# A searched order for the first 640 steps, and products of zeros in nearly all TensorE waits of the opening, in an attention and gated-MLP kernel

## The chip, the core and the metric

One core of a Trainium2 chip runs the whole kernel. The time is device microseconds of one execution; a verdict rests on several executions of both kernels on the same chip. The kernel before took 577.91 us (median of 3 runs, 577.79 to 578.27).

## What is computed

Attention over 8 batches, 8 heads, 576 positions and 64 channels, then a gated MLP on its output, all in float32:

```python
scores = scale * np.matmul(q, k.transpose(0, 1, 3, 2))
mask = (rel >= 0) & (rel < 128)
scores = np.where(mask, scores + bias, -1e9)         # bias = -slope(h) * |rel|
attn = softmax(scores); x = attn @ v                 # heads side by side: 576 x 512
h = gelu_tanh(x @ w_in); u, v = halves of h
v_s = w_sg @ layer_norm(v, g_ln) + b_sg[:, None]     # mixes positions
out = x + (u * v_s) @ w_out
```

The products of the MLP are done in three float32r products each (high by high, high by low, low by high); the weights come as 64-bit words and are first split into a high and a low float32r part.

## The kernel before

The work is cut into named steps. 32 pairs of heads (four of a batch) each go through the same attention steps; the letter is the step, the number is the pair:

- q, L: loads of q and k, and of v, issued by SP
- a, c (for pairs 5 and on together as *): score matmuls of the first and second half (TensorE, line 278)
- A, B, C, G: masks, bias and row minima (VectorE, lines 302 and 295)
- e, E, f, F, j: exponentials (ScalarE, line 311), with their row sums
- R: reciprocals of the row sums (VectorE, lines 322 and 323)
- s, S, r: scaling (ScalarE, line 329, or GpSimd, line 334)
- t, T, z: transposes (TensorE, lines 347 and 360); X, Y: their masked copies (VectorE, line 356); P: a small copy (ScalarE)
- V: products with v (TensorE, lines 384 and 388)
- x, p: gather on ScalarE (line 393); 2: gather on VectorE (line 396; step "22" is pair 2's, "20" pair 0's, "21" pair 1's)
- h, l, k: high and low part of the MLP's input (ScalarE line 401, GpSimd line 218, ScalarE)

The weights w_in are split by six steps each (number 0 to 7; 8 to 11 are w_out): i load (line 181), d on ScalarE (lines 192 and 194), b and o on VectorE (lines 196 and 198), + on GpSimd (line 218), H on ScalarE (line 203), and - on GpSimd (line 218) for even numbers, on VectorE (line 208) for odd ones. wl, wH and w- do the same for w_sg.

Of the MLP of batch 0, the second half of the hidden layer comes first: w20 and its like are the product of position block 2 with the input rows of pair 0, v02 is the last of a block's four (lines 607 to 609, 512 columns wide, reads h and l); vg is its gelu (line 786), nv..., vn... its norm. u000, u001 and so on are the products of the first half (lines 607 to 609, 288 wide), ug0 its gelu, tt0 to tn0 the last 64 positions, y020 and so on the products with w_sg.

W0, W1 and so on are products of zeros: a 128 by 128 block of a tile of zeros times 288 columns of it, into a PSUM buffer that nobody reads.

```python
for i in range(n):
    at = i // len(banks) % 2 * (512 - S2)
    nc.tensor.matmul(banks[i % len(banks)][:, at:at + S2], spare[:, 0:P], spare, start=True, stop=True)
```

The order of all steps is one written list, the table ORDER. A loop at the end takes its steps one after the other and emits their instructions; each engine, and the queue of loads and stores on SP, gets its instructions in this order and runs them in this order. So a step waits for its data and for a free buffer, and everything behind it on its engine waits as well. The buffers that matter here: two of each of three PSUM pools (ps_s, ps_a of one bank, ps_m of two), two of qk, two of vt, four staging buffers for weights (wst).

```python
for n, run in plan.run(ORDER.split()):
    run()
    for i in nc.cur_bb.bb.instructions[before:]:
        if i.engine in last:
            tc.add_manual_dep(i, last[i.engine], ..., reason="order")
        last[i.engine] = i.name
```

Of the kernel before, what the change touches and what calls it, by code (L numbers as in the profile page):

```python
# [21 lines left out]
def attention_gmlp(  # L22
# [26 lines left out]
    S2 = S // 2  # L49
# [8 lines left out]
    IDLE = [(12, "ps_a"), (4, "ps_a"), (4, "ps_s"), (4, "ps_s"), (4, "ps_a"), (4, "ps_m"), (4, "ps_m"), (3, "ps_m"), (4, "ps_m"), (4, "ps_m"), (2, "ps_m"), (2, "ps_m")]  # L58
# [6 lines left out]
    ps_s = ctx.enter_context(tc.tile_pool(name="ps_s", bufs=2, space=PSUM))  # L65
    ps_a = ctx.enter_context(tc.tile_pool(name="ps_a", bufs=2, space=PSUM))
# [100 lines left out]
    gb = const.tile([P, F], F32, name="gb")  # L167
# [978 lines left out]
    for b in range(B):  # L1146
# [4 lines left out]
        q0 i2 d2 i1 q1 a0 c0 A0 a1 i0 B0 C0 G0 b2 c1 e0 d1 E0 F0 j0 f0 d0 b1 o2 o1 +2 A1 R0 B1 C1 b0 o0 G1 L0 i5 q3 i3  # L1151
        j1 H2 s0 E1 e1 f1 r0 F1 d3 S0 +0 +1 -2 W0 t0 X0 W5 T0 Y0 W2 W4 z0 R1 b3 o3 P0 r1 V0 z1 H0 p0 s1 H1 x0 a3 A3 B3
        t1 20 X1 c3 C3 G3 -0 +3 S1 T1 W9 wl2 wH2 P1 w-2 i6 q2 d5 d6 H3 h0 wl3 L1 i7 q5 L2 F3 j3 e3 E3 f3 d7 a2 b5 b6
        o5 +5 l0 Y1 A2 B2 R3 o6 -3 -1 b7 W11 W8 W3 V1 s3 w20 t3 W10 W6 x1 p1 j2 e2 21 h1 +6 S3 X3 c2 l1 w30 T3 W7 w00
        w21 E2 wH3 C2 f2 G2 F2 r3 z3 w-3 H6 P3 Y3 R2 s2 -6 o7 S2 +7 L3 i9 i4 gb i10 V3 x3 23 p3 k1 H5 r2 h3 w01 t2 w10
        T2 X2 Y2 l3 w31 w11 z2 d4 d10 P2 V2 x2 H7 p2 b4 o4 b10 o10 22 +4 +10 w13 w33 *5 A5 B5 C5 G5 w03 w23 h2 H4 d9
        l2 v03 v02 v00 v01 W1 e5 j5 vg03 H10 vg02 vg00 vg01 -5 b9 o9 -7 -4 nv30b nv00b nv10b -10 +9 nv00p u000 u030
        u001 F5 k0 H9 nv10c nv00c -9 E5 nv00h f5 k3 nv30c vn00 L5 i11 q7 i8 wl1 q4 tl R5 a4 u031 A4 B4 s5 t5 nv20b r5
        z5 uc00 wH1 k2 tH uc03 j4 E4 w-1 nv10p S5 nv20p t- e4 nv10h X5 c4 C4 f4 G4 P5 F4 bl L4 wl0 tt0 T5 u020 Y5 R4
        vn01 tj0 s4 r4 u021 V5 t4 nv20c u010 tg0 d11 nt0b nv30p x5 p5 wH0 S4 nt0p w-0 X4 25 T4 z4 u011 Y4 nv20h uc02  # L1160
        nv30h P4 bH nt0c vn03 b- vn02 V4 nt0h x4 d8 p4 uc01 tn0 b11 o11 b8 24 o8 y020 y021 *7 +11 ug0 A7 +8 B7 y000
        y001 H11 j7 H8 Us0 C7 G7 -11 -8 Us1 gm02 gm00 F7 E7 f7 e7 q9 q6 L6 *6 A6 R7 gh00 gh02 h4 B6 C6 e6 q8 L7 s7
        y010 y011 t7 S7 gl02 r7 T7 y030 G6 gm01 X7 F6 E6 f6 j6 R6 gl00 s6 S6 Y7 y031 z7 gm03 gh01 h5 P7 V7 p7 gh03
        gl01 t6 T6 X6 Y6 Oa0 x7 gl03 r6 O00 z6 27 oa00 Us2 l4 l5 P6 h7 V6 p6 x6 Us3 26 O01 h6 l6 l7 *8 oa01 A8 B8 C8
        Us4 G8 u100 u101 e8 *9 E8 f8 j8 F8 R8 A9 B9 u110 s8 S8 r8 t8 C9 k4 k7 Uh1 uc10 E9 j9 f9 e9 k5 k6 Ul1 X8 G9
# [105 lines left out]
```

## Time and profile before

| | |
|---|---|
| time, median of 3 runs | 577.91 us (577.79 to 578.27) |
| the profiled execution, span from first to last instruction | 577.4 us |
| mean granted TensorE clock | 0.997 |
| TensorE matmul busy | 560.8 us, 97%, 5495 matmuls |
| VectorE busy | 473.8 us, 82% |
| ScalarE busy | 378.6 us, 66% |
| GpSimd busy | 308.0 us, 53% |
| the chain that ended last | TensorE 90%, VectorE 5%, DMA 2%, ScalarE 1% |

The page gives the span of the profiled execution and no other time of it; the median of the runs lies 0.5 us over that span. PE is TensorE, DVE is VectorE, ACT is ScalarE, POOL is GpSimd. The granted clock is a share of 2.4 GHz, so 0.50 is 1.2 GHz. In a time line a row gives start, duration, engine, line, operation and tiles, and in brackets the idle time ahead of it with what ended that; matmuls overlap, so a row of several is a little longer than the time to the next row. The opening, up to some 57 us, is where TensorE has idle time and where the products of zeros stand; behind it TensorE is busy nearly throughout.

### The profile page before, as it was taken

What the parts mean: (1) busy time and instruction counts of PE and PEld (TensorE: products, weight loads), DVE (VectorE), ACT (ScalarE), POOL (GpSimd) and SP (SyncE); (2) the same over time, 40 slices, a digit from 0 to 9 for tenths busy, and PEclk for the clock granted to TensorE, in tenths of its full rate; (3) what the DMA queues carried; (4) which work ended last, traced back from release to release, by engine and by line L of the source; (5) the groups of instructions that cost most, each with busy time, mean ns of one, the idle gap of its engine ahead of it and who ended that gap; (6) DMA issues with size and microseconds to landing.
All of it is one profiled execution on the core that took longest, in us unless ns stands there. A gap on an engine that the chain in (4) does not pass through costs nothing.

```text
span 577.4 us, 14654 instructions
## 1 busy us (share of the span) xinstructions
PE 560.8 (97%) x5495; PEld 512.7 (89%) x5495; DVE 473.8 (82%) x1324; ACT 378.6 (66%) x1063; POOL 308.0 (53%) x365
## 2 busy tenths in 40 slices
PE   5889999999999999999999999999999999999997
PEld 4667899998899799997999998998989999998997
DVE  7989998799989868899788987878897988666646
ACT  7988997466853867467776576746695667833422
POOL 3676646530436543575447753496347653576325
PEclk9989999999999999999999999999999999999999
DMA  8675213216403413454260465135332606012502
GB/s 297 190 235 199 72 45 121 69 46 243 167 37 125 156 37 99 146 192 129 60 212 10 140 204 173 43 103 168 130 120 65 214 2 197 2 35 96 171 1 82
DMA packets 43561, 69.78 MB, mean 121 GB/s; under 512 B 3554, under 2 KB 31202, under 8 KB 43492
## 3 DMA queue, kind: packets, MB, share of 16 engines
q1 hardware_dynamic: 43492, 68.86, 36.7%
q8 instruction: 43, 0.70, 0.5%
q14 instruction: 26, 0.21, 0.1%
HBM read 56.27 MB, written 12.58 MB: 119 GB/s over the span
## 4 chain that ended last, share of the span: by engine, by line
PE 90%; DVE 5%; DMA 2%; ACT 1%; issue 1%; POOL 0%; SPq 0%; DVEq 0%; ACTq 0%
PE ps_m L607 13%; PE ps_m L1059 13%; PE ps_m L609 12%; PE ps_m L608 12%; PE ps_m L905 12%; PE ps_a L347 5%; PE ps_s L384 4%; PE ps_s L278 4%; PE ps_a L278 4%; PE ps_m L384 3%; DMA qk<-qkT 2%; PE ps_m L941 2%; PE ps_m L940 1%; DVE px L356 1%; DVE e L295 1%; PE ps_m L796 1%
## 5 line engine op out<-in xcount | busy, mean ns | idle before, releaser
L334 POOL TENSOR_TENSOR e<-e,rr 128x256 f32<-128x256 f32 (+2 forms) x116 | 80.7, 718 | 97.0 <-DVE rr L323 84.9
L311 ACT ACTIVATE e<-e,stats 128x128 f32<-128x128 f32 (+1 forms) x288 | 110.6, 386 | 17.7 <-DVE stats L295 17.1
L224 POOL TENSOR_TENSOR region<-u,region 128x288 fp32r<-128x288 f32 (+1 forms) x78 | 77.7, 1016 | 44.7 <-ACT region L1006 16.2
L356 DVE TENSOR_TENSOR px<-ps_a,m_both 128x1024 f32<-128x1024 f32 x64 | 77.4, 1216 | 5.9 <-PE ps_a L347 5.4
L607 PE MATMUL ps_m<-ws,region 128*128 128x288 f32 x256 | 78.2, 306 | 0.0
L609 PE MATMUL ps_m<-ws,region 128*128 128x288 f32 x256 | 75.7, 296 | 0.0
L608 PE MATMUL ps_m<-ws,region 128*128 128x288 f32 x256 | 75.6, 295 | 0.0
L730 POOL TENSOR_TENSOR rs<-rs,mhalf 128x1 f32<-128x1 f32 (+1 forms) x40 | 30.2, 756 | 57.4 <-DVE rs L727 57.2
L218 POOL TENSOR_TENSOR xs<-xf,xs 128x288 fp32r<-128x288 f32 (+1 forms) x48 | 49.9, 1060 | 13.8 <-ACT xs L401 13.8
L311 ACT ACTIVATION_READ_ACCUMULATOR e<-e,stats 128x1 f32 x288 | 54.4, 189 | 0.0
L1006 ACT ACTIVATE region<-u 128x576 fp32r<-128x576 f32 x35 | 23.7, 684 | 43.4 <-PE ps_m L608 17.4
L607 PEld LDWEIGHTS ps_m<-ws,region 128*128 128x128 f32 x256 | 48.3, 189 | 1.5 <-issue 0.8
L608 PEld LDWEIGHTS ps_m<-ws,region 128*128 128x128 f32 x256 | 48.2, 188 | 0.1
L609 PEld LDWEIGHTS ps_m<-ws,region 128*128 128x128 f32 x256 | 48.1, 188 | 0.1
L607 PE MATMUL ps_m<-wi,xs 128*128 128x512 f32 x112 | 46.9, 418 | 0.1
L1066 DVE TENSOR_TENSOR xf<-ps_m,xf 128x576 f32<-128x576 f32 x48 | 35.7, 750 | 10.9 <-PE ps_m L1059 10.1
L609 PE MATMUL ps_m<-wi,xs 128*128 128x512 f32 x112 | 44.3, 395 | 0.0
L608 PE MATMUL ps_m<-wi,xs 128*128 128x512 f32 x112 | 44.2, 395 | 0.0
L946 DVE TENSOR_TENSOR u<-ps_m,u 128x576 f32<-128x576 f32 x32 | 24.0, 752 | 18.7 <-PE ps_m L941 11.5
L347 PE MATMUL ps_a<-ident,e 128*128 128x128 f32 x256 | 38.0, 275 | 1.0 <-DVE px L356 1.0
L295 DVE CUSTOM_DVE_ANT_0 e<-ps_s,bias 128x128 f32<-128x128 f32 (+1 forms) x140 | 34.9, 287 | 2.5
L278 PE MATMUL ps_s<-qk 64*64 64x192 f32 (+2 forms) x576 | 31.5, 333 | 5.3 <-DMA qk<-qkT 4.9
(217 smaller groups left out, 1600.9 us busy)
## 6 DMA issues: line engine op xcount, KB each, us to landing
qk<-qkT SPq DMA_DIRECT2D x32, 576.0 KB, 4.7
sum<-store SPq DMA_DIRECT2D x36, 512.0 KB, 4.8
outT<-xf SPq DMA_DIRECT2D x31, 288.0 KB, 3.0
vt<-v_in SPq DMA_DIRECT2D x32, 256.0 KB, 4.1
wst<-w_in SPq DMA_DIRECT2D x8, 512.0 KB, 4.8
store<-sum SPq DMA_DIRECT2D x6, 512.0 KB, 2.7
vt<-v_in SPq DMA_DIRECT2D x64, 32.0 KB, 4.2
wst<-w_out SPq DMA_DIRECT2D x4, 512.0 KB, 3.6
```

Of the source, the lines that this page charges most:

```text
L218: (engine or nc.gpsimd).tensor_tensor(out[:, cs], a[:, cs], b[:, cs], op)
L224: nc.gpsimd.tensor_tensor(out[:, fs], a[:, fs], b[:, fs], ALU.subtract)
L278: return lambda: nc.tensor.matmul(banks[half][to, c:c + k1 - k0], qk[js, 0, q0:q0 + R], qk[js, 1, k0:k1], start=True, stop=True)
L311: nc.scalar.activation(x, x, AF.Exp, bias=self.nm[0:n, i:i + 1], scale=-1.0, accum_out=self.sm[0:n, i:i + 1])
L334: nc.gpsimd.tensor_tensor(x[:, z:z + step, :], y[:, z:z + step, :], self.rr[0:n, i + z:i + z + min(k, step)].rearrange("p (m o) -> p m o", ...
L347: burst([lambda t=t: nc.tensor.transpose(cv[:, t // 2, t % 2], self.pr[j][:, t, :].rearrange("p (h c) -> p h c", h=2), ident[:, j * R:j * ...
L356: nc.vector.tensor_tensor(xv, cv, mv, ALU.mult)
L607: nc.tensor.matmul(dst, ah, bh, start=(first and i == 0), stop=False)
L608: nc.tensor.matmul(dst, ah, bl, start=False, stop=False)
L609: nc.tensor.matmul(dst, al, bh, start=False, stop=(last and i == n - 1))
L905: nc.tensor.matmul(dst, left(n, g, c)[:, ms], right(n, h, c), start=first and c == 0 and k == 0, stop=c == 1 and k == 2, skip_group_check= ...
L1059: nc.tensor.matmul(dst, p, q, start=first and f == 0 and k == 0, stop=f == 1 and k == 2, skip_group_check=True)
```

## The change

Two tables change, no step's own code. IDLE says how many products of zeros each W step has and in which pool: 12 steps with 51 products become 24 steps with 85. ORDER puts the first 640 or so steps, up to about 165 us of the span, in another order; the remaining 1363 steps stand as before.

```diff
-    IDLE = [(12, "ps_a"), (4, "ps_a"), (4, "ps_s"), (4, "ps_s"), (4, "ps_a"), (4, "ps_m"), (4, "ps_m"), (3, "ps_m"), (4, "ps_m"), (4, "ps_m"), (2, "ps_m"), (2, "ps_m")]
+    IDLE = [(4, "ps_m"), (4, "ps_m"), (5, "ps_m"), (1, "ps_m"), (4, "ps_a"), (4, "ps_a"), (4, "ps_a"), (4, "ps_a"), (4, "ps_a"), (5, "ps_a"), (2, "ps_m"), (1, "ps_m"), (4, "ps_m"), (4, "ps_m"), (2, "ps_m"), (3, "ps_m"), (4, "ps_m"), (3, "ps_m"), (3, "ps_a"), (4, "ps_a"), (5, "ps_a"), (5, "ps_s"), (4, "ps_s"), (2, "ps_s")]
...
-        q0 i2 d2 i1 q1 a0 c0 A0 a1 i0 B0 C0 G0 b2 c1 e0 d1 E0 F0 j0 f0 d0 b1 o2 o1 +2 A1 R0 B1 C1 b0 o0 G1 L0 i5 q3 i3
+        W10 q0 W15 W11 a0 c0 A0 W6 B0 C0 i2 d2 G0 b2 o2 W19 +2 q1 e0 a1 A1 c1 E0 i1 B1 W8 f0 j0 W5 W9 F0 R0 d1 b1 o1 i0
...
```

Three places, as the built programs have them. First TensorE, from its first instruction to the first transposes of pair 0 (line 347). The matmuls of line 278 are a0, c0, a1, c1; those of line 1139 are zeros. Before:

```order
L278 MATMUL ps_s<-qk 64x64 x2
L278 MATMUL ps_m<-qk 64x192 x8
L278 MATMUL ps_m<-qk 64x128 x2
L278 MATMUL ps_m<-qk 64x192 x6
L278 MATMUL ps_m<-qk 64x64 x2
L278 MATMUL ps_s<-qk 64x192 x8
L1139 MATMUL ps_a<-spare 128x288 x12
L347 MATMUL ps_a<-ident,e 128x2x64 x4
L1139 MATMUL ps_m<-spare 128x288 x4
L347 MATMUL ps_a<-ident,e 128x2x64 x4
```

And in the changed kernel:

```order
L1139 MATMUL ps_m<-spare 128x288 x6
L278 MATMUL ps_s<-qk 64x128 x2
L278 MATMUL ps_s<-qk 64x192 x6
L278 MATMUL ps_s<-qk 64x64 x2
L278 MATMUL ps_m<-qk 64x192 x8
L1139 MATMUL ps_a<-spare 128x288 x8
L278 MATMUL ps_m<-qk 64x128 x2
L278 MATMUL ps_m<-qk 64x192 x6
L278 MATMUL ps_m<-qk 64x64 x2
L278 MATMUL ps_s<-qk 64x192 x8
L1139 MATMUL ps_a<-spare 128x288 x26
L347 MATMUL ps_a<-ident,e 128x2x64 x4
```

Six zeros now precede the first scores, eight stand between c0 and a1, and 26 in place of 12 between c1 and the first transposes; 11 more follow between the two groups of transposes, then 4, 8 and 5 up to a3.

Second, TensorE from the zeros ahead of pair 2's first scores (a2, line 278) to V1 (line 384). Before:

```order
L1139 MATMUL ps_m<-spare 128x288 x4
L278 MATMUL ps_s<-qk 64x128 x2
L278 MATMUL ps_s<-qk 64x192 x6
L278 MATMUL ps_s<-qk 64x64 x2
L1139 MATMUL ps_m<-spare 128x288 x6
L1139 MATMUL ps_s<-spare 128x288 x4
L384 MATMUL ps_s<-px,vt 64x128 x2
L384 MATMUL ps_s<-px,vt 64x192 x12
```

And in the changed kernel:

```order
L278 MATMUL ps_s<-qk 64x64 x2
L607 MATMUL ps_m<-wi,xs 128x512
L608 MATMUL ps_m<-wi,xs 128x512
L609 MATMUL ps_m<-wi,xs 128x512
L607 MATMUL ps_m<-wi,xs 128x512
L608 MATMUL ps_m<-wi,xs 128x512
L609 MATMUL ps_m<-wi,xs 128x512
L607 MATMUL ps_m<-wi,xs 128x512
L608 MATMUL ps_m<-wi,xs 128x512
L609 MATMUL ps_m<-wi,xs 128x512
L384 MATMUL ps_s<-px,vt 64x128 x2
L384 MATMUL ps_s<-px,vt 64x192 x12
```

Ten zeros between a2 and V1 have gone; the products w20, w00 and w10 stand there, which were behind V1.

Third, VectorE from the reciprocals R3 (lines 322 and 323) to the gather 21 (line 396). Before:

```order
L322 TENSOR_SCALAR rr<-stats_126 128x9
L323 RECIPROCAL rr<-rr 128x9
L198 SCALAR_TENSOR_TENSOR tmp<-wst,tmp 128x512
L208 TENSOR_TENSOR wi<-tmp,wi 128x512 x2
L196 TENSOR_SCALAR tmp<-tmp 128x512
L396 TENSOR_TENSOR xf_133<-ps_s,xf_133 128x512
```

And in the changed kernel, where R3 stands 13 rows further up, behind the step o5, and pair 2's minima A2 and B2 (line 295 here) follow it:

```order
L295 ISA e,stats_130<-ps_s,bias_103 128x128
L295 ISA stats_130 128x1
L196 TENSOR_SCALAR tmp<-tmp 128x512
L208 TENSOR_TENSOR wi<-tmp,wi 128x512
L198 SCALAR_TENSOR_TENSOR tmp<-wst,tmp 128x512
L196 TENSOR_SCALAR tmp<-tmp 128x512
L396 TENSOR_TENSOR xf_133<-ps_s,xf_133 128x512
```

Before, o6, -3, -1, b7 and 21 followed R3. Now it is A2, B2, b7, -1, o7, b6 and 21; o6 and -3 come later.

On SP's queue the first loads are now q0 i2 q1 i1 i0 q3 i3 L0 i6 i5 wl2 q2 i7 L1; before they were q0 i2 i1 q1 i0 L0 i5 q3 i3 wl2 i6 q2 wl3 L1. On TensorE the four zeros ahead of u000 (W1) have gone, and the order of the last products of the second half is w13 v01 v00 v03 w23 v02 u000 in place of w03 w23 v03 v02 v00 v01 W1 u000.

## Rows read from the trace of the kernel before

**Rows 1.** Busy time by stretch: from and to, length, busy us (count) by engine, granted clock, DMA share, GB/s

```profile
57.00:79.35 22.35, 22.35 (x239) 20.28 (x239) 21.46 (x58) 20.89 (x60) 14.93 (x16) 1.00 0.23 70
79.35:165.00 85.65, 85.65 (x885) 77.95 (x883) 76.61 (x228) 58.40 (x173) 32.15 (x32) 1.00 0.34 116
```

The engines stand in the order PE matmuls, PE weight loads, DVE, ACT, POOL.

**Rows 2.** Time line of TensorE, around the first product of u000

```profile
55.85 0.69 PE L1139 MATMUL ps_a<-spare 128*128 128x288 f32 x4
56.98 0.40 PE L607 MATMUL ps_m<-xs,wi 128*128 128x288 f32 x1 [0.43 <-ACT xf L786]
57.22 0.30 PE L608 MATMUL ps_m<-xs,wi 128*128 128x288 f32 x1
```

**Rows 3.** Busy time by stretch, up to pair 2's gather

```profile
6.50:22.00 15.50, 12.52 (x148) 10.11 (x140) 14.05 (x59) 14.81 (x57) 7.17 (x6) 1.00 0.82 270
22.00:50.41 28.41, 25.44 (x261) 19.34 (x264) 25.02 (x70) 24.85 (x79) 19.82 (x16) 0.94 0.69 219
```

**Rows 4.** Time line of VectorE: A3, A2, -3 and -1, b7, 23, o10, 22, -5

```profile
21.97 0.30 DVE L302 COPY_PREDICATED ps_s<-sel,ps_s 128x128 f32<-128x128 uint8 x1 [1.00 <-PE ps_s L278]
...
29.37 0.28 DVE L302 COPY_PREDICATED ps_s<-sel,ps_s 128x128 f32<-128x128 uint8 x1
...
32.01 2.38 DVE L208 TENSOR_TENSOR wi<-tmp,wi 128x512 fp32r<-128x512 f32 x2
34.31 1.26 DVE L196 TENSOR_SCALAR tmp<-tmp 128x512 int32<-128x512 int32 x1
...
43.41 0.69 DVE L396 TENSOR_TENSOR xf<-ps_s,xf 128x512 f32<-128x512 f32 x1 [1.97 <-ACT xf L393]
...
48.14 1.67 DVE L198 SCALAR_TENSOR_TENSOR tmp<-wst,tmp 128x512 int32<-128x512 int32 x1
49.73 0.68 DVE L396 TENSOR_TENSOR xf<-ps_s,xf 128x512 f32<-128x512 f32 x1
...
54.33 0.69 DVE L208 TENSOR_TENSOR wi<-tmp,wi 128x512 fp32r<-128x512 f32 x1
```

**Rows 5.** Groups of VectorE, 6.50 to 50.41 us: count, busy us in all, mean ns

```profile
L198 DVE SCALAR_TENSOR_TENSOR tmp<-wst,tmp 128x512 int32<-128x512 int32 x9 | 7.0, 784 | 0.1
...
L196 DVE TENSOR_SCALAR tmp<-tmp 128x512 int32<-128x512 int32 x9 | 4.4, 508 | 0.0
```

**Rows 6.** The stretch of lower clock; TensorE's zeros ahead of it, V1 in it, V3

```profile
31.30:34.70 3.40, 3.40 (x41) 2.94 (x42) 3.37 (x5) 2.81 (x9) 2.53 (x2) 0.50 0.36 108
...
30.49 0.76 PE L1139 MATMUL ps_s<-spare 128*128 128x288 f32 x4 [1.44 <-DVE stats L295]
31.26 2.88 PE L384 MATMUL ps_s<-px,vt 64*64 64x128 f32 x36
...
41.30 1.57 PE L384 MATMUL ps_s<-px,vt 64*64 64x128 f32 x36
```

**Rows 7.** Time line of TensorE: a0, a1, the twelve zeros, the first transposes, a3

```profile
4.86 1.56 PE L278 MATMUL ps_s<-qk 64*64 64x128 f32 x20 [4.86 <-DMA qk<-qkT]
...
9.64 1.56 PE L278 MATMUL ps_m<-qk 64*64 64x128 f32 x20 [1.94 <-DMA qk<-qkT]
...
12.41 2.66 PE L1139 MATMUL ps_a<-spare 128*128 128x288 f32 x12
14.91 0.60 PE L347 MATMUL ps_a<-ident,e 128*128 128x128 f32 x4
...
21.00 0.88 PE L278 MATMUL ps_s<-qk 64*64 64x128 f32 x20
```

**Rows 8.** Time line of ScalarE: s0

```profile
13.78 1.27 ACT L329 ACTIVATE e<-e,rr 128x128 f32<-128x128 f32 x4
```

**Rows 9.** Time line of GpSimd: S3, w-3

```profile
33.80 1.49 POOL L334 TENSOR_TENSOR e<-e,rr 128x512 f32<-128x512 f32 x1
...
38.38 1.43 POOL L218 TENSOR_TENSOR ws<-wst,ws 128x576 fp32r<-128x576 f32 x1
```

**Rows 10.** DMA issues of the first 30 us: count, KB each, median us to landing

```profile
qk<-qkT SPq DMA_DIRECT2D x5, 576.0 KB, 5.9
```

More of the change, by code (lines that the diff above doesn't have):

```diff
@@ L1150, in attention_gmlp @@
     ORDER = """
-        q0 i2 d2 i1 q1 a0 c0 A0 a1 i0 B0 C0 G0 b2 c1 e0 d1 E0 F0 j0 f0 d0 b1 o2 o1 +2 A1 R0 B1 C1 b0 o0 G1 L0 i5 q3 i3
[L1152 to L1165, printed above, removed]
@@ new lines, in attention_gmlp @@
+        W7 j1 W20 q3 C1 e1 W4 G1 i3 s0 r0 t0 X0 W17 S0 d0 +1 b0 W0 W12 E1 T0 Y0 F1 L0 f1 W13 z0 P0 o0 +0 d3 R1 r1 i6 W16
+        i5 W1 V0 p0 b3 wl2 o3 x0 q2 20 H0 W23 s1 +3 W18 z1 a3 A3 W3 -0 S1 B3 t1 d5 X1 b5 e3 c3 C3 wH2 P1 w-2 W14 T1 G3
+        j3 h0 l0 f3 Y1 i7 W2 o5 a2 F3 E3 R3 +5 w20 d7 s3 S3 A2 w00 w10 H1 B2 b7 d6 E2 -1 o7 L1 V1 i10 w30 b6 x1 21 p1 +7
+        t3 X3 W22 H2 -2 c2 C2 G2 j2 T3 r3 z3 o6 Y3 h1 wl3 wH3 l1 w-3 +6 L3 f2 L2 P3 e2 F2 R2 W21 H3 w01 -3 w11 s2 S2 V3
+        x3 23 q5 p3 t2 q4 X2 H6 -6 T2 w21 r2 w31 Y2 h3 d10 b10 i4 d4 z2 bl gb i9 P2 b4 l3 o4 +4 V2 o10 H7 x2 p2 22 w33
@@ new lines, in attention_gmlp @@
+        d9 h2 k0 -7 w03 b9 H5 l2 *5 A5 L4 H4 e5 B5 C5 w13 v01 vg01 v00 vg00 v03 vg03 -5 w23 v02 +10 G5 -4 u000 H10 u001
+        o9 +9 nv00b nv30b nv00p vg02 nv00c f5 wl1 H9 nv10b -10 u030 nv30c nv10c -9 nv00h E5 j5 vn00 tl u031 i8 F5 uc00
+        R5 s5 r5 uc03 k3 tH S5 a4 nv20b u020 wH1 A4 B4 k2 k1 L5 t5 X5 nv20p nv10p q7 E4 c4 t- C4 G4 nv30p T5 e4 nv10h f4
+        wl0 q6 F4 j4 w-1 nv20c u021 z5 P5 Y5 tt0 V5 R4 nv30h s4 vn01 tj0 nv20h vn02 t4 tg0 nt0b nt0c uc02 x5 i11 r4 wH0
+        S4 p5 d8 nt0p nt0h X4 u010 w-0 T4 Y4 u011 z4 P4 25 L6 V4 bH vn03 b- d11 tn0 y020 x4 b8 uc01 p4 24 b11 o11 ug0 *7
@@ new lines, in attention_gmlp @@
+        y330 y331 gh31 j20 E20 p18 h18 gl31 l16 gm32 gt31 e20 F20 f20 k16 gh35 l18 Y19 gm33 gl35 gt32 R20 gt33 *21 A21
+        V19 gh33 x19 O31 gl33 r20 s20 z20 219 gh37 gh36 gh32 P20 O35 t20 oa31 gl36 O36 oa35 B21 C21 oa36 gl32 gt34 gl37
+        O33 O37 oa33 S20 T20 O32 p19 ut45 h19 j21 E21 gh34 k18 f21 oa37 X20 oa32 gl34 O34 l19 uh45 e21 k19 tt4 G21 Y20
+        F21 oa34 tj4 ul45 R21 ut46 tg4 q22 D31 *22 nt4b s21 nt4p S21 L20 D30 D33 D32 V20 x20 nt4c uh46 nt4h lu41 lu40
+        q25 q23 lu42 L21 220 v41 v40 A22 vg41 B22 ut47 uh47 tn4 vg40 r21 z21 U41 t21 U45 ul47 ul46 E22 ue41 U46 C22
@@ new lines, in attention_gmlp @@
+        gh45 gm42 R24 gm43 *25 V23 s24 l21 gl45 S24 O41 A25 gt43 gt42 B25 gh43 x23 k20 j25 h22 gh46 p23 gl43 223 gh42
+        oa41 gl46 t24 T24 O45 C25 oa45 O46 oa46 O43 gl42 gt44 oa43 k21 gh47 gh44 E25 gl47 l22 k22 h23 f25 O47 O42 X24
+        oa47 G25 oa42 gl44 r24 l23 O44 oa44 ut55 k23 z24 tt5 F25 v51 Y24 P24 uh55 e25 tj5 R25 tg5 nt5b ut57 q29 q26 *26
+        nt5c L24 lu50 D40 D41 L25 lu51 q27 D43 lu52 V24 s25 ul55 ut56 A26 vg51 x24 uh57 nt5p nt5h uh56 ul57 ul56 224 tn5
+        v50 vg50 t25 U51 U55 nv05b ut54 B26 nv05c ue51 U56 ue55 uh54 ue56 p24 r25 z25 U53 C26 X25 ue53 U57 ul54 S25
@@ new lines, in attention_gmlp @@
+        ue62 *31 A31 s30 ul64 S30 r30 nv06p B31 V29 nv16h j31 E31 x29 C31 229 t30 U64 T30 v63 X30 nv06c ue64 nv06h p29
+        e31 lo62 lo61 L31 L30 D52 D53 lo60 vn60 Y30 vn61 G31 z30 v62 vg63 nv36b vg62 nv26b nv26c nv36c P30 nv26p nv36p
+        F31 f31 ya610 V30 p30 nv26h nv36h ug6 ya600 ya601 ya611 vn62 R31 vn63 y600 y601 s31 y610 r31 h28 l28 z31 t31
+        y611 gm60 h29 x30 y620 l29 S31 y621 gm61 230 X31 gh61 gl61 gt61 T31 Y31 gm62 y630 y631 gm63 h30 gh65 k29 gh63
+        gt63 gl65 O61 gt62 O65 gh67 P31 V31 gh66 k28 p31 gh62 x31 oa61 gl66 oa65 O66 gl63 gl67 gl62 oa66 231 O63 oa63
```

112 lines of the change are left out of this document (50 added, 62 removed).

## The prediction

> **What bounds the kernel now.** I read the stretches by engine first. From 57.00 to 79.35 us TensorE is busy 22.35 of 22.35 us, from there to 165 us 85.65 of 85.65 [rows 1], and over the whole span 97%. So behind 57 us TensorE alone sets the end, and whatever moves the start of that dense stretch moves the end by as much. The stretch begins with u000, the first product of the gate's input: at 56.98, after four products of zeros and 0.43 us of waiting for ScalarE [rows 2]. The forecast is therefore a forecast of when u000 starts.
>
> Before it, TensorE is not the bound. I read the waits and the time line of VectorE next. It begins pair 0's minima (A0) at 6.50 and ends step 22, the gather of pair 2, at 50.41; in these 43.91 us it is busy 14.05 + 25.02 = 39.07 and idle 4.84 [rows 3]. The large waits are 1.00 for a3 at 21.97 and 1.97 for x3 at 43.41 [rows 4]. Some busy time is loss, too: where a GpSimd instruction was under way, the two L208 (-3 and -1) took 2.38 us and the L196 of b7 1.26, the L198 of o10 1.67 [rows 4]. An L208 alone takes 0.69 [rows 4]; the other eight L196 of the stretch share 4.4 - 1.26 us, 0.39 each, the other eight L198 7.0 - 1.67, 0.67 each [rows 5]. The excess is 1.1 (two follow each other every 0.6), 0.85 and 1.0 us, 2.95 in all. After 22 comes a fixed chain h2, l2, the last v products, gelu, u000: 6.57 us.
>
> Third, TensorE's clock. Between 31.30 and 34.70 the granted clock is 0.50, that is 1.2 GHz [rows 6]. It fell after TensorE had stood idle for 1.44 us up to 30.49 [rows 6]. V1 took 2.88 us there, V3 at 2.4 GHz 1.57 [rows 6]. The first scores ran at the lower level as well: 1.56 us against 0.88 for a3's same twenty matmuls [rows 7]. TensorE had a gap of 1.94 us before a1 (its DMA) and none between a1 and the end of the twelve zeros, in whose run the rate rose: twelve took 2.66 [rows 7], four much later 0.69 [rows 2].
>
> **The change, part by part.** Both orders put the same 51 VectorE steps ahead of 22 and the same 41 TensorE steps, zeros aside, ahead of u000. So I count in three stretches of VectorE and leave the sum of its work alone. The set ahead of A2 (pair 2's first minima, at 29.37 before [rows 4]) is also the same but for R3 in place of b6, 0.4 us each.
>
> *Six zeros ahead of the first scores:* free. They lie in the 4.86 us that TensorE waits for the first load [rows 7]; if the load came at once they would cost six spacings of 0.13, 0.8 us.
>
> *Up to A2.* Between c1's end (12.41, where the zeros start [rows 7]) and a3 TensorE now carries 26 + 11 + 4 + 8 + 5 = 54 zeros, before it carried 24. Zeros are 288 columns wide; four took 0.69 and a single matmul of that width 0.30, so at 2.4 GHz they follow each other every (0.69 - 0.30) / 3 = 0.13 us [rows 2]; the twelve at the start, mostly at 1.2 GHz, took 0.22 each [rows 7]. The useful work there is an estimated 2.9 us: 1.6 for V0, as V3 [rows 6], two groups of transposes of 0.60 with their overlap, 0.4 to the next [rows 7], and 0.5 for two single ones. At full rate 54 zeros with their five changes of type (0.1 each) make 7.7, so a3 starts 10.6 us after c1's end. How early the rate doubles no row of the old order can show. If it is full from the first score, c1 ends near 9.8, but the first transposes must wait for s0, which ScalarE ends at 15.05 now [rows 8]. d0 and H2 no longer stand ahead of s0 and e1 does, some 0.8 us less, so I put its end near 14.3; a3 then comes at 21.3. If it stays low until 14.2, as before (seven spacings of 0.26 and five of 0.13 fill the 2.5 us from 12.41 to the transposes), c1 ends at 12.3, the 26 zeros at 16.5, and a3 comes at 23.6. I take 22.2, between the two: the eight zeros behind c0 fill most of the 1.94 us gap, so the rise should not come later than before. Before, a3 started at 21.00 [rows 7]. VectorE loses those 1.2 us at A3, but has step 20 (0.6) already behind it. **+0.6 us** (-0.3 to +2.2).
>
> The load of pair 2 (q2) now stands on SP's queue behind wl2, which waits for the buffer that +0 frees. +0 follows o0, so I put q2's issue near 21.3; such loads land after 5.9 us [rows 10], at 27.2, and a2 will want it near 27.5. Free, with 0.3 us of cover; beyond it each us is paid. The loads of v0 and v1 move back on the queue as well, with more cover.
>
> *From A2 to 22.* Before, 21.04 us. (a) b7 and -1, the stretched L196 and L208, now follow R3, A2 and B2. +5 and S3 are the GpSimd steps that can be under way, and end about 2.0 us after R3 by my estimate; the next, +7, waits for o7 behind them. So of 1.95 us excess 1.7 goes. (b) V1 no longer follows idle time: w20, w00 and w10 stand ahead of it, 2.2 us of useful products where 1.44 us were idle. If the clock holds, V1 is 1.3 us shorter, and x3's wait of 1.97, which ended a TensorE chain that ran from V1 through w20, c2 and w30 to V3, shrinks; V3 then waits for Y3 and keeps about 0.9. 1.0 goes. (c) o6 now stands where l1 and w-3 follow each other on GpSimd (w-3 took 1.43 [rows 9]). It may wait from nothing to 1.4; I take 0.7. (d) 21 now comes behind b6 and waits for x1, 0.2. **-1.8 us**; the ends are 0 (the same losses at other places) and -5.7 (all of the waits and excess above in this stretch gone).
>
> *From 22 to u000.* The last four zeros go, and w23 moves into the place ahead of v02. From the start of those zeros to u000 1.13 us passed [rows 2]; w23 takes 0.7. **-0.4 us** (0 to -1.1).
>
> *After u000.* TensorE's steps up to the first y product are the same set. VectorE is the near rival there: 21.46 busy of 22.35 [rows 1], and that product reads what VectorE makes last. Both move together, so 0; if VectorE loses more than its 0.9 of idle time there, each us is paid. The new places further on, up to 165 us, lie where VectorE and ScalarE have room: **0** (0 to +1).
>
> The sum: +0.6 - 1.8 - 0.4 = -1.6. Against the profiled execution, 577.4 of span becomes 575.8; the median, 577.91, lies 0.5 over that span, so the runs should show **576.3**.
>
> **A rule weighed.** VectorE was stretched where GpSimd had started first, as b7 beside S3 [rows 4, 9]; o6 is priced at half of the longest such wait. The Trainium skill, "SBUF — State Buffer", section "Who interferes with whom", says that the port pair of the two engines is an exclusive lock and the loser fully blocks. The trace agrees: b7 ended 0.28 us after S3 did [rows 4, 9]. By that rule o6 would pay the whole 1.4 and R3 up to 1.3, and the sum would be about nothing, as the second rival says.
>
> **The rivals.**
> - *More goes than I count* (574.4): also o10's excess of 1.0 and the rest of x3's wait, 0.9, vanish: -3.5. For it speaks that nearly every wait of TensorE is filled, so the clock would hold; against it that o10 again stands right behind o4, which starts +4. Chance 0.17.
> - *GpSimd blocks VectorE at new places* (577.9): R3 stands directly behind o5, whose end starts +5, a product like w-3 [rows 9]; if R3's second half then waits, that is 0.9, and o6 waits 1.4 instead of 0.7. +1.6 takes all. The three stretched steps show that it happens. Chance 0.27.
> - *Zeros at half rate stand ahead of useful work* (579.4, slower). In TensorE's queue the 54 zeros run whether data are ready or not. If the clock rises only at 14.2, a3 is 1.4 later than I take it; if it falls once more in the later waits, as at 31.3, the stretch costs half of its 3.4 us [rows 6], 1.7. Together -1.6 + 3.1 = +1.5. It decides from 2.8 us of such loss. For it: the first scores were at half rate for long, and only 17 zeros cover the waits from a3 on. Against it: one such stretch was there before too. Chance 0.18. The Trainium skill, "TensorE: Matmul & The Clock Gate", Part 1, calls the number of matmuls at half rate at a kernel's start run-variable; one trace here cannot show that.
>
> **How the numbers follow.** The forecast holds 0.38; its own range is 574.9 to 576.7. No change means within 0.2%, 1.16 us, about what the measurement can tell. Faster is the forecast and the first rival, 0.55; same the second, 0.27; slower the third, 0.18. The range goes from 573.5, where most of the first rival ends, to 579.8, just past the third.
>
> **What would show it.** In the new profile u000's first matmul should start near 55.4, and TensorE be dense after it. Step by step: a3 near 22.2; no stretch of granted clock 0.50 around V1; both L208 steps ahead of 22 near 0.69; the gather 22 ending near 49.2; no zeros and no wait of 0.4 ahead of u000. The forecast is wrong if u000 starts after 56.5, if a3 comes after 23, if VectorE shows new long rows of L198 or of R3's L322, or if TensorE has idle time between u000 and 165 us.

## The result, and the profile after

The changed kernel takes 583.76 us (median of 4 runs, 582.78 to 585.33), the kernel before 578.09 on the same chip: the ratio is 1.0101 (95% interval 1.0089 to 1.0113). It is slower by 5.7 us; 576.3 was forecast, so the prediction was wrong in sign. The profiled execution is 4.3 us longer than that of before (581.7 against 577.4).

Two lines of the page of the changed kernel, the busy time of each engine and the shares of the chain that ended last:

```profile
PE 565.8 (97%) x5529; PEld 516.3 (89%) x5529; DVE 478.7 (82%) x1324; ACT 380.0 (65%) x1063; POOL 312.1 (54%) x365
...
PE 88%; DVE 6%; ACT 3%; DMA 2%; issue 1%; POOL 0%; SPq 0%; DVEq 0%; ACTq 0%
```

The shares hardly moved. Where the time went is seen when the span is cut at the steps that the prediction cut it at. Each boundary is the start or end of that step in the two time lines:

| stretch | before | after | change | forecast |
|---|---|---|---|---|
| up to A2 (VectorE) | 29.37 | 29.30 | -0.07 | +0.6 |
| A2 to the end of 22 | 21.04 | 18.57 | -2.47 | -1.8 |
| 22 to u000 (TensorE) | 6.57 | 11.31 | **+4.74** | -0.4 |
| u000 to y020, the first product with w_sg | 22.37 | 24.63 | **+2.26** | 0 |
| y020 to the end | 498.05 | 497.89 | -0.16 | 0 |
| sum | 577.4 | 581.7 | +4.3 | -1.6 |

So the opening, which the forecast was mostly about, did what it should and a little more: 22 ends at 47.87 instead of 50.41. All of that and 4.5 us more are lost in the 36 us behind it. The same stretches on all engines (start and end, length, then busy us and count of TensorE, its weight loads, VectorE, ScalarE, GpSimd, then granted clock, DMA share, GB/s) answer to [rows 1, 3]:

```profile
47.87:50.87 3.00, 3.00 (x42) 2.05 (x42) 2.97 (x5) 1.97 (x5) 2.73 (x3) 1.00 0.38 103
50.87:54.06 3.19, 0.00 (x1) 0.00 (x1) 2.98 (x19) 2.85 (x7) 2.07 (x2) 0.98 0.28 76
54.06:57.00 2.94, 2.93 (x6) 1.83 (x6) 1.60 (x6) 0.60 (x1) 1.29 (x1) 0.50 0.06 22
57.00:59.18 2.18, 1.51 (x7) 1.24 (x7) 1.86 (x7) 1.12 (x2) 1.52 (x2) 0.93 0.73 237
59.18:83.81 24.63, 22.94 (x239) 20.00 (x237) 22.21 (x53) 22.35 (x62) 13.05 (x14) 1.00 0.33 110
83.81:165.00 81.19, 81.19 (x846) 73.76 (x846) 74.22 (x223) 55.55 (x161) 33.66 (x31) 1.00 0.35 112
```

TensorE stands idle from 50.87 to 54.06, then works at a granted clock of 0.50 (1.2 GHz) until 57; u000 comes at 59.18. From 83.81 on it is dense, as before. TensorE's time line there, the changed kernel (start, duration, line, tiles, idle time ahead and what ended it), which answers to [rows 2]:

```profile
50.48 0.39 PE L609 MATMUL ps_m<-wi,xs 128*128 128x512 f32 x1
54.06 0.80 PE L607 MATMUL ps_m<-wi,xs 128*128 128x512 f32 x1 [3.19 <-ACT vg L786]
...
56.36 0.63 PE L609 MATMUL ps_m<-wi,xs 128*128 128x512 f32 x1
57.67 0.50 PE L607 MATMUL ps_m<-wi,xs 128*128 128x512 f32 x1 [0.69 <-ACT xf L786]
...
59.18 0.30 PE L607 MATMUL ps_m<-xs,wi 128*128 128x288 f32 x1
...
82.40 1.41 PE L384 MATMUL ps_s<-px,vt 64*64 64x192 f32 x32 [0.20 <-DVE xf L396]
```

The row at 50.48 is the last of v01, 54.06 the first of v00, 57.67 of w23, 59.18 of u000; 82.40 is the later part of V4, which stands just ahead of y020. v00 waits for line 786, the gelu vg01; w23 for vg03. ScalarE in the same stretch:

```profile
48.69 1.15 ACT L203 ACTIVATE wi<-tmp 128x512 fp32r<-128x512 f32 x2
51.14 0.40 ACT L311 ACTIVATE e<-e,stats 128x128 f32<-128x128 f32 x1 [1.30 <-DVE stats L295]
...
52.02 1.28 ACT L1236 ACT_TABLE_LOAD   x1
...
53.43 0.58 ACT L786 ACTIVATE vg<-ps_m 128x512 f32<-128x512 f32 x1
55.74 0.60 ACT L786 ACTIVATE vg<-ps_m 128x512 f32<-128x512 f32 x1 [1.74 <-PE ps_m L609]
57.02 0.60 ACT L786 ACTIVATE xf<-ps_m 128x512 f32<-128x512 f32 x1 [0.68 <-PE ps_m L609]
...
59.38 0.60 ACT L786 ACTIVATE xf<-ps_m 128x512 f32<-128x512 f32 x1 [1.24 <-PE ps_m L609]
```

vg01 (53.43) stands behind e5 (51.14), which waits 1.30 us for VectorE's minima A5, and behind a table load of 1.28. Then gelu and product wait for each other in turn: 1.74, 0.68, 1.24 on ScalarE, 3.19 and 0.69 on TensorE. And VectorE, first the changed kernel's rows of 22, -7, b9, A5 and nv20c, then GpSimd's +4, l2 and w-1:

```profile
47.19 0.68 DVE L396 TENSOR_TENSOR xf<-ps_s,xf 128x512 f32<-128x512 f32 x1
47.79 1.21 DVE L208 TENSOR_TENSOR wi<-tmp,wi 128x512 fp32r<-128x512 f32 x1
48.92 1.65 DVE L196 TENSOR_SCALAR tmp<-tmp 128x512 int32<-128x512 int32 x1
50.49 0.28 DVE L302 COPY_PREDICATED ps_a<-sel,ps_a 128x128 f32<-128x128 uint8 x1
...
71.43 2.00 DVE L733 SCALAR_TENSOR_TENSOR xf<-xf,mv,gb 128x512 f32<-128x512 f32 x1
```

```profile
46.80 1.64 POOL L218 TENSOR_TENSOR tmp<-tmp,wst 128x512 int32<-128x512 int32 x1 [1.71 <-ACT xf L393]
48.71 1.57 POOL L218 TENSOR_TENSOR xs<-xf,xs 128x576 fp32r<-128x576 f32 x1 [0.27 <-ACT xs L401]
...
71.45 1.43 POOL L218 TENSOR_TENSOR ws<-wst,ws 128x576 fp32r<-128x576 f32 x1
```

b9, begun 0.21 us after l2, ends 0.29 after l2's end, at 1.65 us instead of 0.42; A5, e5 and vg01 follow it. nv20c, 0.95 in the kernel before, begins 0.02 ahead of w-1, takes 2.00 and ends 0.55 after it. -7, too, takes 1.21 instead of 0.69 and ends 0.56 after +4. Two causes are thus on the page: TensorE and ScalarE waiting for each other, and VectorE beside GpSimd. Their sum over the stretch from the end of 22 to the end of tn0 (VectorE's last step that the y products read), the same 87 VectorE instructions in both, first before, then after:

```profile
50.41:81.04 30.63, 30.20 (x308) 26.67 (x298) 28.76 (x87) 29.07 (x79) 18.98 (x19) 1.00 0.30 96
```

```profile
47.87:84.62 36.75, 31.18 (x298) 25.93 (x299) 32.39 (x87) 29.69 (x79) 20.66 (x20) 0.95 0.33 105
```

The stretch is 6.12 us longer: 3.63 of it is VectorE busy longer with the same work, 2.49 is VectorE idle longer.

### The profile page after: what moved, and what is told of

It is laid out like the page before. It is cut to its first block, busy times and chain, and to the rows that moved or that the text cites. A ratio compares the mean times of both kernels' runs of the same rounds, so it can differ in the third digit from the quotient of the medians.

```text
span 581.7 us, 14720 instructions
## 1 busy us (share of the span) xinstructions
PE 565.8 (97%) x5529; PEld 516.3 (89%) x5529; DVE 478.7 (82%) x1324; ACT 380.0 (65%) x1063; POOL 312.1 (54%) x365
## 4 chain that ended last, share of the span: by engine, by line
PE 88%; DVE 6%; ACT 3%; DMA 2%; issue 1%; POOL 0%; SPq 0%; DVEq 0%; ACTq 0%
PE ps_m L1059 13%; PE ps_m L607 13%; PE ps_m L609 12%; PE ps_m L608 12%; PE ps_m L905 12%; PE ps_a L347 4%; PE ps_a L278 4%; PE ps_m L384 4%; PE ps_s L278 3%; PE ps_s L384 3%; DMA qk<-qkT 2%; PE ps_m L941 1%; PE ps_m L940 1%; DVE px L356 1%; PE ps_a L1139 1%; PE ps_m L796 1%
## 5 line engine op out<-in xcount | busy, mean ns | idle before, releaser
L334 POOL TENSOR_TENSOR e<-e,rr 128x256 f32<-128x256 f32 (+2 forms) x116 | 81.9, 731 | 99.3 <-DVE rr L323 72.7
L1059 PE MATMUL ps_m<-region,sum 128*128 128x288 f32 x252 | 36.5, 298 | 0.0
```

The costliest lines, as they stand in the source:

```text
L334: nc.gpsimd.tensor_tensor(x[:, z:z + step, :], y[:, z:z + step, :], self.rr[0:n, i + z:i + z + min(k, step)].rearrange("p (m o) -> p m o", ...
L1059: nc.tensor.matmul(dst, p, q, start=first and f == 0 and k == 0, stop=f == 1 and k == 2, skip_group_check=True)
```

## The experiments

Why does v00 wait for vg01? The four gelus' inputs lie in two PSUM tiles of two banks; v00 writes one half of the tile of which vg01 reads the other (lines 780 and 786). The data need no order between them, but a step that is written behind a read of the same tile waits for it. The kernel before has all four last products ahead of all gelus; the changed order has them in turn: v01 vg01 v00 vg00 v03 vg03 w23 v02, and vg02 further on. w23 writes the other half of the tile that vg03 reads. **Theory A** says that this alternation makes the wait. **B**: ScalarE and VectorE are late anyway, and TensorE with them. **C**: the zeros cost the time. **D**, later: VectorE, not u000, sets the end behind 22. **E**, later: b9 beside l2 decides.

**The products ahead of the gelus.**

```diff
-  v01 vg01 v00 vg00 v03 vg03 -5 w23 v02 +10
+  v01 v00 vg01 vg00 v03 -5 w23 v02 vg03 +10
```

> The changed order with two steps moved: the gelus vg01 and vg03 stand behind the products v00 and v02 that write the other half of the same two-bank PSUM tile. Theory A (shared tile): v00 waited 3.19 us for vg01 (and w23 0.69 for vg03) only because both halves are one tile to the waits; with the products first both waits go, TensorE keeps 2.4 GHz there, the six products run from 50.0 to 53.7, the gelus follow e5 and its table load from 53.4, and u000 starts near 54.5 instead of 59.2. The time falls from 583.8 by 4.7 to 579.1, and to about 577 if VectorE's chain behind it shrinks back by the 2.2 us that it lost as well. Theory B (ScalarE and VectorE are the bound there, whatever TensorE waits for): the gelus still come after e5 and its table load, u000 stays at 57.5 or later and the time above 581.5. Theory C (the zeros cost the time, early): no change, 583 to 584.5.

Measured: 580.3 us (578.16 to 581.21), ratio to before 1.0033 (1.002 to 1.0045). TensorE in the profiled execution (578.16 us, the fastest of the six), first row of v00 and of u000:

```profile
50.47 0.39 PE L607 MATMUL ps_m<-wi,xs 128*128 128x512 f32 x1
...
53.27 0.30 PE L607 MATMUL ps_m<-xs,wi 128*128 128x288 f32 x1
```

No wait ahead of either, at 2.4 GHz throughout. v00 began 1.36 us before vg01 did (51.83), so it did not need it: A holds for the wait, and u000 comes 5.9 us earlier than in the changed kernel, 3.7 earlier than before. C falls. But the time is not below that of before: y020 starts at 78.26, only 1.1 earlier than before. The gain in u000 is given back behind it, which speaks for a part of B.

**The exponential behind the gelus**, alternation kept (first), and with the products first (second):

```diff
-  H4 e5 B5 C5 w13 v01 vg01 v00 vg00 v03 vg03 -5
+  H4 B5 C5 w13 v01 vg01 v00 vg00 v03 vg03 e5 -5
```

```diff
-  H4 e5 B5 C5 w13 v01 vg01 v00 vg00 v03 vg03 -5 w23 v02 +10
+  H4 B5 C5 w13 v01 v00 vg01 vg00 v03 -5 w23 v02 vg03 e5 +10
```

> The changed order with one step moved: the exponential e5 stands behind vg03, so that vg01 waits neither for A5 nor for a table load behind e5; gelus and products still alternate. Theory A: half of the loss stays, since each product still waits for the gelu of the other half: vg01 ends near 51.9 instead of 54.0, v00 waits 1.0 instead of 3.19, w23 some 0.7, u000 starts at 56 to 57, and the time is 580 to 581.5, slower than with the products first. Theory B: the lateness of the gelus was all of it, and this edit does as well as or better than the one with the products first, 577 to 579. Theory C: no change.

> Both edits: products v00 and v02 ahead of the gelus, and e5 behind vg03. Theory A: u000 starts as early as l2 (GpSimd, done at 50.3) and the six products allow, at 53.7 to 54.3, half a us or so ahead of the run with the products first alone; 576 to 579. Theory B: as the run with e5 moved alone. If the early e5 served something that now comes late (j5, R5, X5), up to 1 us worse than with the products first alone.

Measured: 581.98 us (1.0057; 1.0042 to 1.0072) and 582.71 (1.0073; 1.006 to 1.0085). The first did to v00 what was expected (wait 0.97, w23 0.69, u000 at 55.75), but its time is 0.5 us above the expected range. Both have a flaw as experiments: vg02 stands behind e5 now, so ScalarE loads the exponential's table, the gelu's and the exponential's again, and R5 comes at 64.15 and 64.31 against 60.89 with the products first alone. The expectation of the second missed by 3.7 us; it left these loads out, and a wait of 2.23 us for vg02 in the middle of the u products, behind which the granted clock is 0.65 from 59.13 to 63.00. What follows: one exponential ahead of vg02 cost two more table loads, 1.28 us each. And u000 does not decide the end here: it is 2.18 us earlier in the second run than in the first (53.57), y020 is 0.17 later (82.91), as R5 is.

**The alternation put into the kernel before**, nothing else:

```diff
-  l2 v03 v02 v00 v01 W1 e5 j5 vg03 H10 vg02 vg00 vg01
+  l2 e5 j5 v01 vg01 v00 vg00 v03 vg03 H10 v02 vg02 W1
```

> The kernel before with nothing but its last products and gelus put in the changed kernel's alternation: v01, vg01, v00, vg00, v03, vg03, v02, vg02 in place of v03, v02, v00, v01 and then the gelus; e5 and j5 ahead of them in both. Theory A: v00 waits for vg01 behind e5 and the table load (before, the first gelu ended at 55.9), some 2 us, v02 for vg03 about 0.7, with TensorE at 1.2 GHz behind the long wait; u000 starts at 59 to 60 instead of 57, and the time is 580.5 to 583, 2.5 to 5 us slower than before. Theories B and C: no loss, within 0.6 us of before.

Measured: 581.94 us (1.0057; 1.0035 to 1.0078), 3.4 slower than before. Its waits on TensorE, v00 and v02:

```profile
55.14 0.50 PE L607 MATMUL ps_m<-wi,xs 128*128 128x512 f32 x1 [2.06 <-ACT vg L786]
...
58.19 0.79 PE L607 MATMUL ps_m<-wi,xs 128*128 128x512 f32 x1 [0.69 <-ACT xf L786]
```

Both as expected; u000 comes at 60.60, 0.6 later than that. The alternation alone costs 3.4 us by the medians, in an order that is otherwise the old one. A is shown from both sides. The 3.4 is the middle of two groups, though: three executions took 580.17 to 580.77 at a mean granted clock of 1.000, three 583.11 to 583.47 at 0.994, the kept trace among them, where the granted clock is 0.50 from 56.00 to 62.60. By the medians of the groups (580.44 and 583.34) 1.9 us come without a fall of the clock and 2.9 more with it. Only one trace was kept, so that split rests on the mean clocks.

**The two halves of the change apart.** The new order and zeros up to 22, then the old rest; and the old order and zeros up to 22, then the new rest (each step once; bl stays at its old place in the first).

```diff
-  [new order up to 22] [new order behind 22]
+  [new order up to 22] [old order behind 22]
```

```diff
-  [old order up to 22] [old order behind 22]
+  [old order up to 22] [new order behind 22]
```

> The changed kernel's order up to the gather 22, with its zeros (the load bl excepted), and everything behind it in the order of the kernel before, without zeros. Theory A (the loss is all behind 22; the opening gained 2.5 us): 22 ends near 47.5 against 50.4 before, the four last products stand together ahead of the gelus, u000 starts near 54.0 to 54.5 against 57.0, VectorE's chain keeps its order and the whole moves by 1.5 to 2.5 us: 576 to 577 us. Theory D (VectorE, already busy throughout behind 22, sets the end there, so an earlier u000 is given back): u000 as early, y020 within 0.7 us of before's 79.35, and 577.5 to 578.5. Theory C (zeros and the opening cost the time): 580 or more.

> The order of the kernel before up to the gather 22, with its zeros, and everything behind it in the changed order, where gelus and last products alternate. Theory A: 22 ends at 50.4, as before, and the whole loss is there, plus the gain of the opening that is gone: u000 at 61 to 62, the time 584 to 587. Theory C: as before or little more, 578 to 580.

Measured: **576.6 us** (576.39 to 577.3; ratio 0.9972, 0.9962 to 0.9983) with the new opening alone, 581.69 (1.0056; 1.0043 to 1.0069) with the new rest alone. The opening is worth 1.8 us, and this version beats both kernels, as A expected. D, by which y020 would have stayed near 79.35 and the time at 577.5 or more, fails in this order. Its u000 and y020:

```profile
54.10 0.40 PE L607 MATMUL ps_m<-xs,wi 128*128 128x288 f32 x1 [0.69 <-ACT xf L786]
```

```profile
77.15 0.40 PE L607 MATMUL ps_m<-ws,region 128*128 128x288 f32 x1
```

2.88 and 2.20 us earlier than before. From 22's end to tn0's it needs 31.30 us, 0.67 more than before; with the products first it was 31.74:

```profile
47.54:78.84 31.30, 29.95 (x304) 26.13 (x303) 28.89 (x86) 29.28 (x79) 20.29 (x20) 1.00 0.29 96
```

```profile
47.33:79.07 31.74, 30.22 (x298) 25.39 (x299) 30.70 (x87) 29.39 (x80) 21.41 (x20) 1.00 0.39 121
```

The first is the new opening with the old rest, the second the run with the products first: there VectorE is busy for 1.8 us more. With the new rest D does hold, and the traces give a reason. In all nine kept traces with it the part of V4 that stands ahead of y020 waits 0.20 or 0.21 us for VectorE's gather 25 (in the changed kernel the row at 82.40), and y020 starts 1.47 us after 25 ends. In the five traces with the old rest TensorE has no such wait, and y020 comes 3.43 us after 25. So with the new rest TensorE takes its pace there from VectorE; with the old one an earlier u000 is mostly kept (2.20 of 2.88 us).

The new rest behind the old opening was 2.3 us faster than the lower end of what was expected: in its trace b9 took 0.41, v00 waited 1.49 instead of 3.19, no fall of the clock followed, and nv20c took 1.10 instead of 2.00. So the two halves do not add up: they are worth -1.8 and +3.3 us apart, and the whole change costs 5.7, some 4 more than their sum.

**The products first, once more**, the same kernel, and **all zeros left out** of it:

```diff
-    IDLE = [(4, "ps_m"), (4, "ps_m"), (5, "ps_m"), ...]
+    IDLE = []
```

> The kernel with the products first once more, unchanged, for a second profiled execution: the first had a span of 576.3, the other five executions 578.1 to 579.4. If the 2 us between them lie in VectorE's instructions beside GpSimd (b9 and nv20c took 1.65 and 2.00 us in the changed kernel, 0.42 and 1.19 in the first execution with the products first), this one shows such long rows between 47 and 80 us and y020 at 79.5 to 81; if they lie in the clock of the opening or in the first load, 22 ends later than 47.3 by as much.

> The order of the run with the products first, with all 85 products of zeros left out (they compute nothing that is read). Theory A with the prediction's view (zeros hide in waits and keep TensorE at 2.4 GHz): TensorE runs at 1.2 GHz through much of the first 45 us, each set of products with v takes 2.9 instead of 1.6 us, 22 ends 1.5 to 4 us later, and the time is 1 to 4 us above the run with the zeros, 581 to 584. Theory C (the zeros stand in front of useful work): the same or up to 1 us faster than with them, 579 to 580.5.

Measured: 579.24 us (one execution), y020 at 79.73, 1.47 later than in the first. 0.6 of it is there at the end of 22 (first load landed 0.47 later), and b9, 0.42 in the first execution, took 1.65 again. In the first it had begun 0.15 us ahead of l2, here 0.19 after it (48.78). So one and the same program falls on either side of this. Without zeros: 582.34 us (1.0071; 1.0051 to 1.0091), 2.0 more than with them, as expected; 22 ends at 48.62.

**b9 out of l2's way**, in the changed kernel and with the products first:

```diff
-  w03 b9 H5 l2 *5 A5 L4 H4 e5 B5 C5 w13
+  w03 H5 l2 *5 A5 L4 H4 e5 B5 C5 b9 w13
```

> The changed kernel with one step moved: b9 (VectorE, line 196) stands behind C5 instead of ahead of A5. In the changed kernel it took 1.65 us, begun 0.21 us after l2 on GpSimd and ended 0.29 after l2's end; in one execution with the products first it began 0.15 us ahead of l2 and took 0.42. Theory E (VectorE loses to a GpSimd instruction that started first, and this row passes its 1.2 us on to A5, e5, vg01 and v00): A5 starts at 48.9 instead of 50.5, vg01 ends near 52.5 to 52.8 instead of 54.0, v00's wait falls from 3.19 to about 1.9, y020 starts 1.0 to 1.5 us earlier, and the time is 582.2 to 582.8 instead of 583.8. Rival: the minima A5, B5, C5 beside l2 are then stretched in its place: no change.

> The order with the products first, and b9 behind C5 as well. Of its two profiled executions the one with b9 at 1.65 us had y020 1.47 us later than the one with 0.42. Theory E: b9 is short in all executions now, and the median falls from 580.3 to 578.6 to 579.3. Rival (the spread of those executions has another cause): 580 to 580.5.

Measured: 582.12 us (1.0063; 1.005 to 1.0075) and 580.16 (1.0036; 1.0023 to 1.0048). In the changed kernel it is the expected gain (v00's wait is 1.78), although -5 took 1.75 us there instead of 0.69; nv20c took 0.92. With the products first it gains nothing, and its trace shows why. VectorE's -5 and nv20c, then GpSimd's -4, nv30p and w-1:

```profile
51.66 1.79 DVE L208 TENSOR_TENSOR wi<-tmp,wi 128x512 fp32r<-128x512 f32 x1
...
67.78 2.52 DVE L733 SCALAR_TENSOR_TENSOR xf<-xf,mv,gb 128x512 f32<-128x512 f32 x1
```

```profile
51.40 1.50 POOL L218 TENSOR_TENSOR wi<-tmp,wi 128x512 fp32r<-128x512 f32 x1
...
67.81 0.55 POOL L730 TENSOR_TENSOR rs<-rs,mhalf 128x1 f32<-128x1 f32 x1
68.33 1.42 POOL L218 TENSOR_TENSOR ws<-wst,ws 128x576 fp32r<-128x576 f32 x1
```

b9 is short, -5 takes 1.79 instead of 0.69, and nv20c 2.52. The loss moved to other steps. So theory E, that b9 alone is the cause, falls; what counts is the sum of such meetings. Counting each VectorE step's excess over its shortest in any trace, from the end of 22 to tn0: 0 in the kernel before, 0.2 in the new opening with the old rest, 3.2 in the changed kernel, 1.9, 2.8 and 4.0 in the three traces with the products first. (-7 begins just ahead of 22's end and adds 0.5 to each of the last four.) The spans of the best version and of the three with the products first are 574.7, 576.3, 577.4 and 578.3, against 0.2, 1.9, 2.8 and 4.0 of excess: nearly us for us. Four traces make it likely that these meetings are what the products first still lose; they do not show it for every execution.

**Two changes to the best version.** The scores of pair 5 ahead of two products, and no zeros:

```diff
-  w13 w33 *5
+  *5 w13 w33
```

```diff
-    IDLE = [(4, "ps_m"), (4, "ps_m"), (5, "ps_m"), ...]
+    IDLE = []
```

> The new opening with the old rest (576.6), and the scores of pair 5 ahead of the products w13 and w33 on TensorE. VectorE stood idle there for 0.83 us ahead of A5, after which it is busy nearly without a gap up to tn0. Theory D (VectorE sets the end behind 22): A5 comes 0.8 us earlier, R5 and tn0 as well, y020 0.4 to 0.8 earlier than 77.15, and the time is 575.8 to 576.3. Theory A alone (u000 sets the end): u000 waits for the gelus behind e5 and j5, which come earlier too, but it cannot start before v01 ends at 53.4, so at most 0.6 us; if the two products now come late for v03 and v01, no gain or a loss up to 0.5.

> The new opening with the old rest, with all products of zeros left out (they compute nothing that is read). With the products first the 85 zeros were worth 2.0 us (582.3 without, 580.3 with). If that holds here, 578.2 to 579, about the time of before: then the gain of the opening is the zeros' and not the new order's. If the new order carries it, 576.6 to 577.5.

Measured: 577.43 us (0.9985; 0.9977 to 0.9994) and 579.7 (578.15 to 583.08; 1.0037, 1.0018 to 1.0056). In the first A5's wait went from 0.83 to 0.03, and -5 from 0.91 to 1.73: no gain, a loss of 0.8, which neither theory expected. u000 (54.99) is 0.89 later and 22's end (47.97) 0.43, so this run does not decide between them. In the second the gain of the opening is gone: the zeros are worth 3.1 us there by the medians. Its twelve executions fall into two groups, seven of 578.15 to 580.23 at a mean granted clock of 0.990 or 0.991, five of 581.37 to 583.08 at 0.985 to 0.988; the kept trace (578.3) is of the first and shows 1.7 us of the loss. The old opening was not run without its 51 zeros, nor the new order with those, so what the new order is worth apart from its zeros is not shown. Windows from 14 to 22 us, with zeros and without:

```profile
14.00:22.00 8.00, 7.71 (x101) 7.07 (x99) 7.86 (x20) 7.21 (x26) 2.80 (x4) 1.00 0.40 132
```

```profile
14.00:22.00 8.00, 5.93 (x53) 4.03 (x56) 7.62 (x19) 6.11 (x22) 2.77 (x4) 0.50 0.39 126
```

Without them TensorE had stood idle for 4.06 us up to 13.53, the granted clock is 0.50 after it, and 22 ends at 48.50 instead of 47.54.

## Why the prediction was wrong

- **The bound.** "Whatever moves the start of that dense stretch moves the end by as much" failed. u000 to y020 took 22.37 us before, 24.63 in the changed kernel, 24.99 with the products first (first trace), 23.05 in the best version. From y020 on the rest is 497.5 to 498.1 in all four. The dense stretch has to be counted from y020, behind VectorE's chain, since VectorE, 21.46 of 22.35 busy [rows 1], is as near a bound. The text named it as the near rival and then let "both move together". They nearly do in the old rest; in the new one y020 follows VectorE's 25.
- **Six zeros: free.** Right: a0 starts at 4.79.
- **Up to A2, +0.6.** Better, -0.07, and within the range. The rate rose in the eight zeros behind c0 (2.20 us from 7.56 on), and a1 took 0.88 us (9.70), before 1.56 [rows 7]; a3 started at 21.38, near the 21.3 given for the full rate. In one of two later traces of the old opening a1 took 0.88 as well.
- **q2's load: free.** Right: issued at 21.29, and a2 starts at 26.83 without a wait.
- **A2 to 22, -1.8.** Right in sign, -2.47; VectorE was busy for 1.16 us less and idle for 1.31 less. b7 and -1 took 0.70 and 0.69, as (a) said; -3 (1.49) and b10 (0.77) took their place in part. (b) rested on one execution: the granted clock of 0.50 at V1 [rows 6] is not in two other executions of the same opening, the alternation put into the kernel before and the old opening with the new rest. They have 1.00 there after nearly the same wait (1.45 and 1.44 us), and 22 ends at 49.58 and 49.64 instead of 50.41. Against these two the stretch is 1.79 shorter, which is the forecast's size, but from other terms: (c) o6 did not wait at all (0.69; w-3 beside it took 1.92 instead of 1.43), o10's excess went, (d) 21 waited 0.74, and x3's wait fell from 1.97 to 0.36, not by 1.0. (b) tied that wait to V1's clock, and wrongly: in the two executions V1 took 1.57 us and x3 still waited 1.86. The opening's worth at 22's end is nearer 1.7 to 2.1 us, and 1.8 in the runs.
- **From 22 to u000, -0.4: the step that failed.** Measured +4.74. The prediction took "a fixed chain h2, l2, the last v products, gelu, u000" and looked at which steps stand in it, not at how gelus and products follow each other. With the products first the same stretch is 5.94 us, 0.2 less than forecast (6.67 in the second trace, where b9 was long); the alternation adds 3.19 of wait, 1.4 of v00 and v03 at 1.2 GHz (2.93 instead of 1.56), and 0.69 of wait.
- **After u000, 0: failed.** +2.26. The price was named ("if VectorE loses more than its 0.9 of idle time there, each us is paid"), but no place was looked for. R5 is 2.26 later than before, behind vg02 and its table load, about as late as u000. From R5 to tn0's end VectorE then needs 1.32 us more (19.41 instead of 18.09), 1.05 of it nv20c beside w-1; and y020 stands 0.81 us ahead of tn0's end instead of 1.69, behind V4's wait for 25. TensorE, which before had no wait between u000 and y020, has four, 1.69 us in all.
- **The rivals.** "GpSimd blocks VectorE at new places" was the right mechanism at the wrong places, and too small: b9, nv00c and nv20c were stretched, R3 and o6 were not. R3's second half ran in 0.22 us although +5 had begun 0.04 us ahead of it. By the Trainium skill, "SBUF — State Buffer", section "Who interferes with whom", the loser of the shared port pair fully blocks; the rows of b9 and l2 agree. "More goes than I count" was half right up to 22: o4 and o10 took 1.29 together, and x3 waited 0.36. "Zeros ahead of useful work" is wrong: leaving them out costs 2.0 and 3.1 us. The clock did fall, but behind v00's wait, not in the opening.
- **The base.** Of 12 later executions of the kernel before, of 577.85 to 579.86 us, each has a span 1.75 to 2.34 us below its time. The 0.5 between 577.91 and 577.4 compares different executions: the profiled one must have been a long one, near 579.2 by an estimate from that difference. So the medians differ by 5.7, the profiles by 4.3.

What stays open: how much of the 3.7 us between the products first (580.3) and the best version (576.6) each single meeting on VectorE costs, and why the two halves together cost some 4 us more than apart; the traces show where (v00's wait, the clock behind it, nv20c), not each share. That the meetings differ between executions of one program is shown by two traces; that they make all of its spread of 3 us is not.

## What to carry to other kernels

Read a reordering for what shares a buffer, not only for what needs whose data: a product written behind the read of the other half of its tile waits for that read (3.19 us here), and with all products first, then all reads, that wait is gone. Try the halves of a large change apart early: here one was worth -1.8 us and the other +3.3, and the whole +5.7, so they need not add up. Where two engines are both near busy, look for the last wait ahead of the dense stretch and count from the engine that ends it, and expect a step moved out of one meeting to run into the next. Where the executions of one kernel fall into groups of different mean clock, a median between them describes neither.

## What was not expected of the hardware

The same opening, after the same idle time on TensorE (1.44 and 1.45 us), ran V1 at a granted clock of 0.50 in one execution [rows 6] and at 1.00 in two others. The old opening with the new rest, the same window:

```profile
31.30:34.70 3.40, 3.34 (x50) 2.87 (x51) 3.40 (x5) 3.40 (x13) 2.61 (x2) 1.00 0.46 140
```

And a VectorE instruction that meets GpSimd can lose to more than one: nv20c, begun 0.07 us ahead of the end of t-, ended 0.55 us after w-1, behind t-, nv30p and w-1 in a row, 2.52 us instead of 0.95.
